# Taking GpSimd out of the last stores of an attention + MLP kernel

## The chip, the core and the metric

The kernel runs on one core of one Trainium2 chip. The metric is device time in microseconds (us) of that core, as the median of several executions. One further execution was recorded by the profiler. The engines are TensorE (PE, with its weight loads shown as PEld), VectorE (DVE), ScalarE (ACT), GpSimd (POOL) and SyncE (SP). SP, ACT and POOL can each issue DMA transfers.

## The reference

For 8 batches of 8 heads, 576 rows and head size 64, a Nystrom form of attention is computed. Its result, 4608 rows of 512, goes through a two-layer perceptron.

```python
q_lm = q.reshape(B, H, m, S // m, D).mean(axis=3)      # m = 32 landmarks
k_lm = k.reshape(B, H, m, S // m, D).mean(axis=3)
A = sm(q, k_lm); Bm = sm(q_lm, k_lm); C = sm(q_lm, k)  # scaled softmaxes
Z = Bm.transpose(0, 1, 3, 2) / (norm_1(Bm) * norm_inf(Bm) + 1e-06)
for _ in range(6):
    Z = 2 * Z - Z @ Bm @ Z
attn_out = A @ Z @ C @ v
x = attn_out.transpose(0, 2, 1, 3).reshape(B * S, H * D)
h = x @ w_in                                           # 4608 x 2048
out = (h * sigmoid(h)) @ w_out                         # 4608 x 512
```

## The kernel before

The kernel works batch by batch. For batch `b`, `attn(b)` builds the landmark softmaxes, the iteration for Z and a matrix `m` that already holds Z, C, v and `w_in`. `layer1(b)` multiplies `etn` (the normalised A) with `m`, 128 hidden columns at a time (`h0` to `h15`), and puts silu of the result into `gm` on ScalarE. Sixty-four of the 576 rows do not fit the 512-wide tile. They are gathered by two narrower groups per batch, `hx0` and `hx8`, each 16 matmuls of 64 columns, and their silu (`gx0`, `gx8`) goes to the tile `gx`. One `gx` holds four batches, so it is complete only when the two groups of the fourth batch are done.

`layer2_batch(b)` multiplies by `w_out`. Two blocks of 256 rows of `gm` are each done by `layer2_pair`, a seven-product scheme. The products are `p1` to `p7`, each 8 matmuls. DVE forms four sums of inputs beforehand (line 1028, tiles `ss` and the second half of the input). The results are collected in two output tiles `ost`, a low one and a high one, by copies and additions (`c1`, `c11`, `u2`, `c22`, `c12`, `c5`, `c21`). `p6`, `p7` and `p4` follow `p1` in its PSUM bank, each after the one before it has been read out (`c1`, `u2`, `c22`). The low tile needs `c11` (after `p2`) and `c12`; the high one `c21` (after `p4`) and `c22` (after `p7`). After batches 3 and 7 a third pair, the one on `gx`, follows. In batch 7 it is the end of the kernel.

Stores: each output tile holds four blocks of 32 rows, and each block goes out as one DMA of 64 KB (line 1005). Everywhere but in the last pair SP issues all of them. In the last pair (`spread`) they are single steps. The high tile goes in eight half stores of 32 KB that SP or ACT may issue, the low tile in four stores of 64 KB that SP, ACT or POOL may issue.

The order of everything is not written out. Each step is an `Op` with the engines that can do it, a planned duration, its dependencies and a rank `prio`, and `Plan.run` builds a list schedule when the kernel is built: at each event it gives an idle engine the ready step with the lowest rank that finds a PSUM bank. The engines then run these lists in order, synchronised by semaphores, so the plan fixes an order, not times. Ranks are 1000 + 100b + column for layer 1 (a half more for `hx`), and 5000 + 100b (+20, +40 for the second and third pair) for layer 2. The step name ends in that number, as in `p2@5740.0`. The dictionary `ORDER` at the top adds a shift to the rank of single steps; `hx0.6` is the group `hx0` of batch 6.

After the last step the Tile framework closes the program. SP waits for the semaphores of all transfers, every engine executes a DRAIN, and GpSimd collects the engines' signals, clears the semaphores and releases them. These instructions carry line 1185.

Of the kernel before, what the change touches and what calls it, by code (L numbers as in the profile page):

```python
# [29 lines left out]
    "m3.5": (1570.1, 0), "p2@5400.0": (14.101, 0), "p4@5400.0": (-0.02249, 0),  # L30
    "Ax11.6": (-36.172, 0), "Cx10.6": (565.87, 0), "p6@5500.0": (-0.10422, 0),
    "ltr1.7": (-211.67, 0), "pbs.7": (230.47, 0), "bbd.7": (541.69, 0), "Rs0.7": (163.07, 0),
    "etn1.7": (-1755.9, 0), "p2@5740.0": (89.123, 0),
}


# [277 lines left out]
def kernel(  # L314
# [9 lines left out]
    nc = tc.nc  # L324
# [84 lines left out]
    A = P.add  # L409
# [563 lines left out]
    ost_st = {}  # L973

    def layer2_plain(gm, c, deps, places, prio):

        pieces = []
        for h in range(2):
            cell = {}
            cols = slice(c + 128 * h, c + 128 * h + 128)  # L980
            for qt in range(4):
                def f(e, qt=qt, cell=cell, cols=cols):
                    for dc in range(4 * qt, 4 * qt + 4):
                        mm(bank(cell["o"]), gm[:, dc, cols], w_out_sb[:, dc, :], start=(dc == 0),
                           stop=(dc == NDC - 1))
                d = deps(4 * qt, 4 * qt + 4) + [wo_ops[qt]]
                o = A(f"o{qt}@{prio + h}", [("PE", mm_us(512, 4))], f,
                      d + ([(pieces[-1], 0.0)] if qt else []), prio + h + 0.01 * qt,
                      psum=0 if qt else 1, cls="L2")
                cell.setdefault("o", o)  # L990
                pieces.append(o)
            i = nost[0] % 6
            nost[0] += 1
            t = ost_r[i]
            a = A(f"oc@{prio + h}", either(512), lambda e, t=t, cell=cell: copy(
                e, t, bank(cell["o"])), [pieces[-1]] + ost_st.get(i, []),
                500.0 + prio / 100).reads(cell["o"])
            ost_st[i] = [A(f"os@{prio + h}", [("SP", 2.2)],
                           lambda e, t=t, h=h: [store(e, t, places[h], m) for m in range(4)],
                           [a], prio, dma=0.65, lag=3.5)]  # L1000
        return pieces

    def store(e, t, place, m, cols=slice(0, DMODEL)):
        b, j = place[m]
        {"SP": nc.sync, "ACT": nc.scalar, "POOL": nc.gpsimd}[e].dma_start(  # L1005
            out=out[b * S:(b + 1) * S, cols].rearrange("(l j) n -> j l n", j=J)[j],
            in_=t[L * m:L * m + L, cols])

    def layer2_pair(gm, c, deps, places, prio, parts=1, spread=False):
# [29 lines left out]
        def prod(nm, i, lhs, rhs, deps, own=None):  # L1039
            cell = {"o": own}  # L1040

            def f(e):
                ps = bank(cell["o"])[:, 0:HM]
                for dc in range(HC):
                    mm(ps, lhs[:, dc], rhs[:, dc], start=(own is None and dc == 0),
                       stop=(dc == HC - 1))
            o = A(f"{nm}@{prio}", [("PE", mm_us(HM, HC))], f, deps, prio + 0.01 * i,
                  psum=1 if own is None else 0, cls="L2")
            o.margin = 0.1
            o.pair = n  # L1050
            if own is None:
                cell["o"] = o
            pieces.append(o)
            return o
# [17 lines left out]
        p2 = prod("p2", 1, a12, b21, [p1] + deps(HC, NDC) + w2)  # L1072
# [16 lines left out]
        for i, t, h, dep in ((lo_i, lo_t, 0, [c11, c12]), (hi_i, hi_t, 1, [c21, c22])):  # L1089
            if spread and h:  # L1090
                ost_st[i] = [A(f"os{u}{m}@{prio + h}", [("SP", 0.45), ("ACT", 0.45)],
                               lambda e, m=m, t=t, u=u: store(e, t, places[1], m, slice(
                                   HM * u, HM * u + HM)), [dep[u]], prio + 0.1 * u,
                               dma=0.1, lag=1.5) for u in range(2) for m in range(4)]
            elif spread:
                ost_st[i] = [A(f"os{m}@{prio}", [("SP", 0.45), ("ACT", 0.45), ("POOL", 0.7)],
                               lambda e, m=m, t=t: store(e, t, places[0], m), dep, prio,
                               dma=0.1, lag=1.5) for m in range(4)]
            else:
                ost_st[i] = [A(f"os@{prio + h}", [("SP", 2.2)],  # L1100
                               lambda e, t=t, h=h: [store(e, t, places[h], m) for m in range(4)],
                               dep, prio, dma=0.65, lag=3.5)]
        return pieces

    def layer2_batch(b):
        l2_last["m", b] = []
        for p in range(2):
            x = (gm_r[b % 2], 256 * p, lambda d0, d1: gm_ops[b][d0:d1],
                 [[(b, j) for j in range(8 * c + p, 8 * c + p + 7, 2)] for c in range(2)],
                 5000.0 + 100 * b + 20 * p)  # L1110
            if b or p:
                l2_last["m", b] += layer2_pair(*x)
            else:
                l2_last["m", b] += layer2_plain(*x)
                w_sums(l2_last["m", b][:])
        if b % 4 == 3:
            l2_last["x", b // 4] = layer2_pair(
                gx_t, 0, lambda d0, d1: [gx_ops[x][d // 8] for x in range(b - 3, b + 1)
                                         for d in range(d0 // 8 * 8, d1, 8)],
                [[(x, j) for x in (y, y + 1) for j in (J - 2, J - 1)] for y in (b - 3, b - 1)],  # L1120
                5000.0 + 100 * b + 40, 1, b == B - 1)
# [68 lines left out]
```

## Time and profile before

| | |
|---|---|
| median of 9 runs | 253.29 us (252.84 to 254.27) |
| profiled execution: its own time | 254.27 us |
| its span, first to last instruction of the program | 252.6 us (252.57) |
| PE / ACT / DVE / POOL busy | 96% / 72% / 68% / 15% |
| mean granted TensorE clock | 0.995 |

The profile is of one execution, which was the slowest of the nine. 1.70 us of its time lie outside its span. Busy shares are averages over the whole span. In groups of instructions, the numbers after the bar are total busy time in us, the mean duration in ns, and the idle time before with what ended it. In the view of one source line, a row gives the duration in ns as minimum, median and maximum, and the first and last start in us. A "q" after an engine's name marks its sequencer (issues of transfers, waits, drains), which is not counted as busy.

### The profile page before, as it was taken

To read this page: it belongs to the slowest core of one execution; us is meant where nothing else is said; L and a number is where in the kernel's file an instruction comes from. 1 tells how busy PE (TensorE), PEld (TensorE's weight loads), DVE (VectorE), ACT (ScalarE), POOL (GpSimd) and SP (SyncE) were. 2 spreads that over 40 slices of the span, in tenths; PEclk is the share of its full clock that TensorE was granted. 3 is DMA by queue.
4 is the path that set the end of the run, shared out by engine and by line. 5 is a ranking of instruction groups with operands and counts; after the bars stand their busy time and mean duration, and the time that the engine had idled before them with its cause. 6 is when DMAs were issued, how large, how long until landed. Compare 5 with 4: busy or idle time off the path is not lost.

```text
span 252.6 us, 7198 instructions
## 1 busy us (share of the span) xinstructions
PE 241.4 (96%) x2846; PEld 173.4 (69%) x2846; DVE 170.9 (68%) x432; ACT 182.3 (72%) x429; POOL 37.8 (15%) x64
## 2 busy tenths in 40 slices
PE   7899999999989999999999999999999999999980
PEld 6777665556867754567886665788776685788870
DVE  2376766596879867949999674399996465257520
ACT  2598997499866999997768889678679977622210
POOL 8436724200040022001300130000000000000000
PEclk9999999999999999999999999999999999999997
DMA  6999999997989799994996999764340023033342
GB/s 104 205 193 199 204 207 208 206 239 124 163 164 214 123 187 193 162 166 93 171 239 136 207 167 215 133 136 114 84 110 0 22 67 83 0 86 84 86 108 58
DMA packets 52465, 35.73 MB, mean 141 GB/s; under 512 B 33376, under 2 KB 43872, under 8 KB 52432
## 3 DMA queue, kind: packets, MB, share of 16 engines
q0 software_dynamic: 15296, 18.42, 43.9%
q1 hardware_dynamic: 36800, 16.56, 30.4%
q8 instruction: 22, 0.36, 0.6%
q10 hardware_dynamic: 336, 0.30, 0.4%
q14 instruction: 11, 0.09, 0.1%
HBM read 36.70 MB, written 9.44 MB: 183 GB/s over the span
## 4 chain that ended last, share of the span: by engine, by line
issue 41%; PE 39%; DMA 9%; ACT 4%; DVE 2%; POOL 2%; SPq 1%; POOLq 0%; DVEq 0%; ACTq 0%
PE ps L392 37%; DMA qT<-qk 6%; DMA qk<-in_q_dram 3%; PE ps L566 2%; SPq L590 1%; DVE red L626 1%; ACT ln L778 1%; POOL v L458 1%; ACT ln L782 1%; PE ps L828 1%; ACT ct L402 1%; ACT et L768 1%; ACT L940 1%; POOL qk L451 0%; POOL qk L445 0%
## 5 line engine op out<-in xcount | busy, mean ns | idle before, releaser
L392 PE MATMUL ps<-etn,m 128*128 128x64 bf16 (+1 forms) x512 | 69.4, 286 | 0.1
L940 ACT ACTIVATE gm<-ps 128x512 f16<-128x512 f32 x128 | 66.1, 659 | 2.3 <-PE ps L392 2.1
L392 PEld LDWEIGHTS <-gm 128*128 128x128 f16 x512 | 48.2, 98 | 11.4 <-issue 2.6
L392 PE MATMUL ps<-w_out_sb,gm 128*128 128x256 f16 (+1 forms) x392 | 53.5, 281 | 0.0
L392 PEld LDWEIGHTS <-m 128*128 128x128 bf16 x512 | 32.5, 98 | 24.8 <-issue 2.6
L402 ACT COPY ost<-ps 128x256 f32<-128x256 f32 (+1 forms) x55 | 21.4, 389 | 32.1 <-PE ps L392 30.6
L392 PEld LDWEIGHTS <-ss 128*128 128x128 f16 x408 | 39.0, 98 | 7.2 <-issue 1.1
L1063 DVE TENSOR_TENSOR ost<-ost,ps 128x256 f32<-128x256 f32 x51 | 21.3, 418 | 23.3 <-PE ps L392 18.3
L392 PE MATMUL ps<-wt,ss 128*128 128x256 f16 x272 | 34.1, 273 | 0.0
L738 DVE SCALAR_TENSOR_TENSOR st<-st,ps 128x320 bf16<-128x320 bf16 (+3 forms) x54 | 21.6, 407 | 8.6 <-PE ps L392 8.3
L404 DVE CAST m<-ps 128x512 bf16<-128x512 f32 x31 | 20.0, 684 | 5.0 <-PE ps L392 4.5
L402 ACT CAST m<-ps 128x512 bf16<-128x512 f32 x33 | 17.8, 600 | 3.5 <-PE ps L392 3.5
L392 PE MATMUL ps<-w_out_sb,ss 128*128 128x256 f16 x136 | 17.6, 273 | 0.0
L451 POOL DMA_DIRECT2D qk<-in_k_dram x7 | 5.0, 717 | 82.2 <-DMA qT<-qk 37.9
L813 ACT ACTIVATE ce<-ps 128x288 bf16<-128x288 f32 x32 | 12.8, 412 | 5.2 <-PE ps L392 5.2
L392 PE MATMUL ps<-zer 128*128 128x256 bf16 x94 | 15.2, 296 | 1.1 <-DVE zer L485 1.1
L458 POOL DMA_DIRECT2D v<-in_v_dram x24 | 14.0, 592 | 14.9 <-PE ps L392 8.6
L392 PE MATMUL ps<-wt,gm 128*128 128x256 f16 x120 | 15.6, 273 | 0.0
L1005 POOL DMA_DIRECT2D out_dram<-ost x1 | 0.5, 528 | 98.8 <-DVE ost L1063 98.8
L392 PE MATMUL ps<-st 128*128 128x160 bf16 (+1 forms) x96 | 14.4, 225 | 0.4 <-DVE st L738 0.3
L1028 DVE TENSOR_TENSOR ss<-gm 128x1024 f16<-128x1024 f16 x15 | 10.2, 686 | 5.2 <-ACT gm L940 5.2
L626 DVE TENSOR_TENSOR red<-qT 128x1024 f16<-128x1024 bf16 x12 | 8.3, 689 | 7.9 <-DMA qT<-qk 7.4
(91 smaller groups left out, 339.7 us busy)
## 6 DMA issues: line engine op xcount, KB each, us to landing
out_dram<-ost SPq DMA_DIRECT2D x137, 64.0 KB, 1.8
v<-in_v_dram POOLq DMA_DIRECT2D x24, 192.0 KB, 12.2
qk<-in_k_dram POOLq DMA_DIRECT2D x7, 576.0 KB, 8.2
qk<-in_q_dram POOLq DMA_DIRECT2D x7, 576.0 KB, 11.6
w_out_sb<-in_moe_w_out_dram POOLq DMA_DIRECT2D x4, 512.0 KB, 10.5
w_in_sb<-in_moe_w_in_dram POOLq DMA_DIRECT2D x4, 256.0 KB, 9.1
w_in_sb<-in_moe_w_in_dram POOLq DMA_DIRECT2D x8, 128.0 KB, 7.3
qk<-in_k_dram POOLq DMA_DIRECT2D x2, 288.0 KB, 4.2
```

The costliest lines, as they stand in the source:

```text
L392: nc.tensor.matmul(out=out_ap, lhsT=lhsT, rhs=rhs, start=start, stop=stop, skip_group_check=True)
L402: nc.scalar.copy(out=out, in_=in_)
L404: nc.vector.tensor_copy(out=out, in_=in_)
L451: lambda e, t=t, src=src: nc.gpsimd.dma_start(out=qk_r[b % 2][:, t].rearrange("p g j d -> p g (j d)"), in_=src[b].rearrange("(g h) (l j) d ...
L458: lambda e, a=a: nc.gpsimd.dma_start(out=v_r[b % 2][a * L:(a + 1) * L, :, :], in_=v[b].rearrange("h (l a x) d -> a l h (x d)", l=L, a=VA)[ ...
L566: nc.tensor.transpose(out=ps[:, n * 128:(n + 1) * 128], in_=qk[:, t, g, 2 * jp:2 * jp + 2, :].rearrange("p j d -> p (j d)"), identity=idb)
L626: lambda e: nc.vector.tensor_tensor(out=o_, in0=a_, in1=b_, op=OP.add),
L738: nc.vector.scalar_tensor_tensor(out=s2[:, g0:g1, lo:SW], in0=s[:, g0:g1, lo:SW], scalar=2.0, in1=ps[:, 0:NG * SW].rearrange("p (g x) -> p ...
L813: nc.scalar.activation(out=ce[:, :, 0:VP].rearrange("p (i c) (a l) -> p c a i l", c=2, a=VA)[:, c], in_=bank(me["C"], 2 * g + c)[:, 0:HS]. ...
L940: lambda e, dc=dc, cell=cell: nc.scalar.activation(out=gm[:, dc, :], in_=bank(cell["o"]), func=AF.Silu),
L1028: lambda e, o_=o_[:, k], x=x[:, k], y=y[:, k], op=op: nc.vector.tensor_tensor(out=o_, in0=x, in1=y, op=op), dep, 850.0 + prio / 100)
L1063: nc.vector.tensor_tensor(out=out_, in0=x, in1=y, op=OP.add)
```

## The change

Two things are done in the diff. The low tile's four stores of the last pair may be issued by SP or ACT only; GpSimd is struck from the list of choices and from `store`. In `ORDER`, the step `hx0.6` gets a shift of 4199.5, so its rank goes from 1607.5 to 5807.0.

```diff
@@ ORDER
     "ltr1.7": (-211.67, 0), "pbs.7": (230.47, 0), "bbd.7": (541.69, 0), "Rs0.7": (163.07, 0),
-    "etn1.7": (-1755.9, 0), "p2@5740.0": (89.123, 0),
+    "etn1.7": (-1755.9, 0), "hx0.6": (4199.5, 0), "p2@5740.0": (89.123, 0),
 }
@@ store
         b, j = place[m]
-        {"SP": nc.sync, "ACT": nc.scalar, "POOL": nc.gpsimd}[e].dma_start(
+        {"SP": nc.sync, "ACT": nc.scalar}[e].dma_start(
             out=out[b * S:(b + 1) * S, cols].rearrange("(l j) n -> j l n", j=J)[j],
             in_=t[L * m:L * m + L, cols])
@@ layer2_pair
             elif spread:
-                ost_st[i] = [A(f"os{m}@{prio}", [("SP", 0.45), ("ACT", 0.45), ("POOL", 0.7)],
+                ost_st[i] = [A(f"os{m}@{prio}", [("SP", 0.45), ("ACT", 0.45)],
                                lambda e, m=m, t=t: store(e, t, places[0], m), dep, prio,
                                dma=0.1, lag=1.5) for m in range(4)]
```

## The prediction

> **What bounds the kernel now.** I read the page first, for what bounds the body, and then only the end, where the change lies: the timeline of the last engines, the closing line 1185, and the busy time in the last microseconds.
>
> ```profile
> span 252.6 us, 7198 instructions
> ...
> PE   7899999999989999999999999999999999999980
> ...
> PEclk9999999999999999999999999999999999999997
> DMA  6999999997989799994996999764340023033342
> ...
> L1005 POOL DMA_DIRECT2D out_dram<-ost x1 | 0.5, 528 | 98.8 <-DVE ost L1063 98.8
> ```
>
> The PE row is at nine tenths or more up to the last slices: the body is bound by TensorE, at full clock. The last row says that GpSimd issues exactly one of the stores, after having had nothing to do for 98.8 us.
>
> ```profile
> 242.16 0.37 ACT L402 COPY ost<-ps 128x256 f32<-128x256 f32 x1 [0.50 <-PE ps L392]
> ...
> 244.58 1.04 PE L392 MATMUL ps<-w_out_sb,gx 128*128 128x256 f16 x8
> 244.78 0.42 DVE L404 COPY ost<-ps 128x256 f32<-128x256 f32 x1 [0.45 <-PE ps L392]
> 245.65 0.42 DVE L1063 TENSOR_TENSOR ost<-ost,ps 128x256 f32<-128x256 f32 x1 [0.45 <-PE ps L392]
> 246.36 0.53 POOL L1005 DMA_DIRECT2D out_dram<-ost  x1 [98.80 <-DVE ost L1063]
> ```
>
> This is the timeline's end (start, length, engine). TensorE's last product ends at 245.6, the last addition (c11, on DVE) at 246.07, and then the low tile's four stores go out: ACT at 246.1, POOL at 246.36, SP at 246.5, ACT at 246.6. All arithmetic is over 6.5 us before the span is. What fills these 6.5 us is in the view of line 1185:
>
> ```profile
> L1185 SPq EVENT_SEMAPHORE  x11: 17/28/683, 246.9 to 252.5; - x11
> L1185 POOLq EVENT_SEMAPHORE  x4: 17/17/17, 251.8 to 252.5; - x4
> L1185 POOLq DRAIN  x3: 46/102/5445, 246.3 to 252.3; - x3
> L1185 SPq DRAIN  x3: 7/7/7, 249.1 to 252.0; - x3
> ```
>
> and in the busy time of the last stretches (PE, PEld, DVE, ACT, POOL, clock, DMA share, GB/s):
>
> ```profile
> 246.00:248.00 2.00, 0.00 (x0) 0.00 (x0) 0.07 (x1) 0.00 (x0) 0.53 (x1) 1.00 0.61 166
> 248.00:250.00 2.00, 0.00 (x0) 0.00 (x0) 0.00 (x0) 0.00 (x0) 0.00 (x0) 1.00 0.14 45
> 250.00:252.60 2.60, 0.00 (x0) 0.00 (x0) 0.00 (x0) 0.00 (x0) 0.00 (x0) 0.50 0.00 0
> ```
>
> SP waits for all transfers and reaches its DRAINs at 249.1 and 249.2. GpSimd's first DRAIN starts at 246.3, with the issue of its store, and lasts 5.445 us, to 251.8; only then come its semaphore instructions (first start 251.8) that release everybody. From 250 on no engine and no DMA does anything. So SP is ready at 249.2 and the core waits 2.6 us more, for GpSimd alone. The chain of waits does not show this: it ends at GpSimd's issue at 246.34, since it follows program work. GpSimd's other two DRAINs in that row took 0.102 and 0.046 us, and one at the program's head, on line 1174, 0.184 us. None of these follows a store by GpSimd.
>
> **The change, part by part.**
>
> GpSimd's store is removed. With it goes the 2.6 us: GpSimd's instruction before it is then its last load, issued by 147.57, and the DRAIN follows that. Bounds on when it ends: with the same 5.4 us, at 153; if it has to outlast the landing of these loads (12.2 us in the page's list of issues) by as much as it outlasted the store's landing (issue 246.36 plus 2.2 is 248.6; 251.8 is 3.2 later), at 163. Both are over 80 us before it is needed. From then on SP's second DRAIN is the last to come. After it I put what followed GpSimd's DRAIN before: 251.8 to 252.57, 0.8 us.
>
> The store is added to SP or ACT. Four stores of 64 KB on two queues are two each, so the added one stands behind another: SP's started at 246.5 and the next can start at about 246.94, since such issues take 0.42 us (median of SP's rows at the end) with some 0.04 between. Nothing waits behind it: ACT's last copy ran at 242.16, SP has only the closing waits. The bytes are the same, and the DMA share of 0.61 and then 0.14 has room. From issue to landing 64 KB took 1.8 us in the page's median and 2.4 at the most in the last 10 us, so it lands between 248.7 and 249.3. Before, the last landing was 248.95 (246.55 + 2.4), and SP's DRAIN came 0.25 later. This way SP would be done at 249.0 to 249.6.
>
> A rule speaks against this part. The Trainium skill, Perfetto Trace Analysis, section DMA Optimizations, says that where descriptor generation is the bottleneck, spreading DMAs over SP, ACT and GpSimd may help; here the stores do stand in a row. By the rule alone the change costs one issue, +0.4 us. By the trace it saves 2.6 and costs that 0.4: GpSimd's issue ended at 246.9 (246.36 + 0.53), no earlier than the last of the others at 247.0. I go with the trace.
>
> hx0.6 is moved. Its 16 matmuls (slots of about 0.47 us, as seen at 200.00 to 200.47) and one silu of 0.6 us (line 963) are the same work elsewhere. Removed near 194.8, they let the rest come 0.47 earlier. By its rank of 5807 it loses to every product of layer 2 but p2@5740.0 (5740.01 + 89.12), so it fills the first moment at which nothing else is ready. That is, I read, behind p1 of the pair 5720: there the trace before has p1 of the last pair at 234.10 (`w_out_sb,gx`), pulled ahead between two products of the other pair because nothing else was ready. But that p1 reads gx, which now lacks gx0.6. So hx0.6 takes this place (233.63 to 234.10), p2 of pair 5720 follows at 234.10, and p1 of the last pair comes after p4 of 5720, at 239.34. The products are 0.87 us each throughout, so seven of them end at 245.45, within the overlap of the pipeline where they ended before: cost zero, if no gap opens.
>
> The cover for that zero: gx0.6 at 234.2 to 234.8 on ACT, then four sums on DVE of 0.69 each (line 1028), 2.8 us, between the additions of pair 5720, so until about 238.5; p5, the first that needs a sum, starts at 240.2. And the three hand-overs in p1's bank (PE to ACT or DVE to PE, 0.09 + 0.42 + some 0.1, so 0.6) need a product of 0.87 between them: p1, p5, p6, p3, p7, p2, p4 is such an order, and the ranks give it. Without cover, each costs up to 0.6.
>
> With that order p4 comes last, not p2, since p2 fills the hand-over before p4. Then the low tile's 64 KB stores start already at 245.25, and the last four are halves of 32 KB, started from 246.1 in two rows of two, the last at 246.57. These land 1.6 us later in the trace, and up to 2.2 if they meet the big ones: 248.2 to 248.8, SP done at 248.4 to 249.05.
>
> The sum: SP done at 248.4 to 249.6 over both orders; I take 249.0, where they meet. Plus 0.8 gives a span of 249.8, against 252.57: 2.8 less. The profiled execution would take 254.27 - 2.8 = 251.5, but it was 0.98 above the median of the runs shown, so I set the gain against the median: 253.29 - 2.8 = 250.5.
>
> **The rivals.**
>
> The DRAIN is not the store's (slower). GpSimd pays 5.4 us of closing that can only begin once the last store of any engine is issued. Then it moves from 246.34 to the end of the added issue, 247.36 (246.94 + 0.42), ends at 252.8, 1.0 later than now: 254.3. It decides as soon as the DRAIN starts later than 246.34; it costs the gain in part as soon as it ends after 249.2. For it: the trace has only one long DRAIN, and it does coincide with the end. Against: it began before the stores of SP at 246.5 and ACT at 246.6 were issued, and the short ones. Chance 0.07.
>
> TensorE waits for the late gx. If hx0.6 falls behind the products of pair 5720, p1 stands until gx0.6 is there: 0.09 + 0.6 + 0.1, 0.8 us, and the sums may add a hand-over of 0.6 or so. Gain 2.8 - 1.4: 251.9 (251.3 with the 0.8 alone). For it: the rank is nearly the lowest of all. Against: the gap at 234.10. Chance 0.12.
>
> The semaphore of the added store is not free. Stores share a few semaphores, and before, SP stood 1.5 us in one such wait (`DMA out_dram<-ost: 1.5`, in SP's list of waits near the end). In the last row that puts the landing off by up to 1.2 us: 251.7. Chance 0.08.
>
> The change does not do what it says: the planner might hand the steps to queues otherwise, but no store can go to GpSimd any more; I give that no share.
>
> **How the numbers follow.** The likeliest case, the DRAIN out of the way and TensorE's end unmoved, has 0.71; its own range is 249.9 to 251.1 (SP done from 248.4 to 249.6). The two cases that eat part of the gain reach to 251.9 with 0.20; 0.07 lies at 254.3, and 0.02 at no change (a disorder that eats it all). For 8 in 10, with 0.2 added to both sides for the spread of medians, the range is 249.8 to 251.9. A measurement of this kernel can tell 0.2%, 0.5 us, from no change. Faster by more than that 0.91, within 0.02, slower 0.07.
>
> **What would show it.** Right: no GpSimd row on line 1005; a long or short GpSimd DRAIN that starts near 147, and its semaphore instruction within 0.1 us of SP's second DRAIN, near 249; the span's last stretch without work shrunk from 3.4 us to 0.8; 20 stores by SP and ACT from 239.9 on, where there were 19 and one by GpSimd; hx0.6 between p1 and p2 of pair 5720 near 233.6; PE's last product ending at 245.6 within 0.2. Wrong: a GpSimd DRAIN of some 5 us still at the end; an idle stretch before a PE product after 234 with `ACT gx` or `DVE ss` as the releaser; an SP semaphore wait of over 0.5 us before the last store.

## The result, and the profile after

| | before | after |
|---|---|---|
| median | 253.14 us (54 runs) | 250.96 us (17 runs) |
| ratio, with its 95% interval | | 0.9903 (0.9887 to 0.9919) |
| profiled execution: its time | 254.27 us | 251.53 us |
| its span | 252.57 us | 249.42 us |
| TensorE's last product ends | 245.61 us | 245.44 us |
| from there to the end of the span | 6.96 us | 3.98 us |
| its time outside the span | 1.70 us | 2.11 us |

The median is 0.46 us above the forecast of 250.5 and inside its range. The ratio is that of the means, 253.22 us before and 250.77 after: a gain of 2.46 us. The medians lie 2.18 apart.

Two rows of the changed kernel's page first, then its timeline of TensorE at the end (start, length, engine):

```profile
span 249.4 us, 7196 instructions
...
PE   8899999999989999998999999999999999999993
...
PEclk9999999999999999999999999999999999999998
```

```profile
233.46 0.63 PE L392 MATMUL ps<-etn,m 128*128 128x64 bf16 x16
...
238.30 1.04 PE L392 MATMUL ps<-w_out_sb,gx 128*128 128x256 f16 x8
239.17 1.04 PE L392 MATMUL ps<-wt,gm 128*128 128x256 f16 x8
...
244.41 1.04 PE L392 MATMUL ps<-w_out_sb,gx 128*128 128x256 f16 x8
```

TensorE is as full as before. hx0.6 (the 16 matmuls of 64 columns) runs at 233.46. p1 of the last pair follows at 238.30, one place ahead of p4 of the pair before it (239.17), and p2 is still the last product (244.41). Now the closing line 1185:

```profile
L1185 SPq EVENT_SEMAPHORE  x11: 17/28/28, 247.1 to 249.4; - x11
L1185 POOLq EVENT_SEMAPHORE  x4: 17/17/17, 248.7 to 249.3; - x4
L1185 POOLq DRAIN  x3: 51/102/16132, 146.1 to 249.1; - x3
L1185 SPq DRAIN  x3: 7/7/13, 248.6 to 248.9; - x3
```

GpSimd's long DRAIN starts at 146.1, with the issue of its last loads, and lasts 16.132 us, to 162.2, when nobody waits for it. SP's second DRAIN comes at 248.6, and GpSimd's semaphore instruction right after it, at 248.7. Before, 2.6 us lay between the two. SP's second DRAIN is now 0.77 us from the end of the span (248.65 to 249.42), where it was 3.36 (249.21 to 252.57). The busy time of the last stretches (columns as before: length, PE, PEld, DVE, ACT, POOL, clock, DMA share, GB/s) has no stretch of 2.6 us without any transfer any more; the last store lands at 248.50:

```profile
246.00:248.00 2.00, 0.00 (x0) 0.00 (x0) 0.00 (x0) 0.00 (x0) 0.00 (x0) 1.00 0.70 186
248.00:249.40 1.40, 0.00 (x0) 0.00 (x0) 0.00 (x0) 0.00 (x0) 0.00 (x0) 0.50 0.01 1
```

SP itself is also earlier: 3.21 us after TensorE's end (248.65 - 245.44) where it was 3.60 (249.21 - 245.61). The list of stores from 240 on says why:

```profile
L1005 SPq DMA_DIRECT2D out_dram<-ost x12: 314/401/435, 239.8 to 246.8; - x12
L1005 ACTq DMA_DIRECT2D out_dram<-ost x6: 374/410/435, 243.4 to 246.4; - x6
...
DMA to landing us min/median/max: 1.5/1.7/1.9
```

The last store is issued later (246.8, before 246.6), but no store takes more than 1.9 us to land; before it was up to 2.4.

### The profile page after: what moved, and what is told of

Read it like the earlier page. It is cut to its first block, busy times and chain, and to the rows that moved or that the text cites. A ratio compares the mean times of both kernels' runs of the same rounds, so it can differ in the third digit from the quotient of the medians.

```text
span 249.4 us, 7196 instructions
## 1 busy us (share of the span) xinstructions
PE 241.7 (97%) x2846; PEld 173.8 (70%) x2846; DVE 169.6 (68%) x430; ACT 182.8 (73%) x431; POOL 37.2 (15%) x63
## 3 DMA queue, kind: packets, MB, share of 16 engines
q0 software_dynamic: 15264, 18.35, 44.5%
## 4 chain that ended last, share of the span: by engine, by line
PE 86%; DMA 6%; ACT 3%; DVE 2%; issue 1%; POOL 0%; DVEq 0%; POOLq 0%; ACTq 0%
PE ps L392 83%; DMA qT<-qk 4%; DMA qk<-in_q_dram 3%; PE ps L566 2%; ACT ln L778 1%; DVE red L626 1%; ACT ln L782 1%; PE ps L828 1%; ACT ct L402 1%; ACT et L768 1%; ACT L940 1%; POOL qk L445 0%; DVE ost L1063 0%; ACT gm L940 0%; DVE ost L404 0%
## 5 line engine op out<-in xcount | busy, mean ns | idle before, releaser
L392 PE MATMUL ps<-etn,m 128*128 128x512 bf16 (+1 forms) x512 | 69.3, 286 | 0.1
L402 ACT COPY ost<-ps 128x256 f32<-128x256 f32 (+1 forms) x57 | 22.1, 388 | 33.8 <-PE ps L392 32.2
L392 PE MATMUL ps<-zer 128*128 128x256 bf16 x94 | 15.8, 304 | 1.1 <-DVE zer L485 1.1
L778 ACT ACTIVATE ln<-ps 128x288 f32<-128x288 f32 x32 | 12.0, 435 | 1.9 <-PE ps L392 1.7
```

What stands on the lines that cost most here:

```text
L392: nc.tensor.matmul(out=out_ap, lhsT=lhsT, rhs=rhs, start=start, stop=stop, skip_group_check=True)
L402: nc.scalar.copy(out=out, in_=in_)
L778: lambda e, g=g, c=c, ln=ln: nc.scalar.activation(out=ln[:, c], in_=bank(me["S", g, c])[:, 0:HS], func=AF.Ln),
```

## Which part of the change earns it

The end of TensorE differs by up to 2.3 us between profiles (243.7 to 246.0). The cause lies in the body, the part up to TensorE's last product, and was not looked for. So the variants are read by two lengths that hardly vary in kernels that share their end: the tail, from TensorE's last product to the end of the span, in the profile; and the time outside the span, device time less span, of every execution. Spans are recorded to 0.1 us, so a single time outside is good to 0.05. Each ratio is to executions of the kernel before that were made beside the variant. GpSimd kept awake has three executions, and the two with the late copy behind an added DRAIN and the kernel before with an early DRAIN have two each; the others have 4 to 17.

| kernel | tail, us | outside the span, us | ratio to before (95%) |
|---|---|---|---|
| before | 6.96 | 1.65 to 1.78 | |
| after | 3.98 | 2.06 to 2.16 | 0.9903 (0.9887 to 0.9919) |
| only hx0.6 moved | 6.95 | 2.08 to 2.16 | 1.0019 (0.9994 to 1.0045) |
| only GpSimd struck | 4.14 | 1.70 to 1.73 | 0.9893 (0.9846 to 0.9940) |
| GpSimd's store one pair earlier | 3.97 | 2.09 to 2.13 | 0.9903 (0.9869 to 0.9936) |
| late GpSimd copy | 6.36 | 2.06 to 2.15 | 0.9993 (0.9966 to 1.0020) |
| late copy, GpSimd kept awake | 6.49 | 2.04 to 2.07 | 0.9955 (0.9923 to 0.9987) |
| early DRAIN, late copy | 3.97 | 2.11 to 2.12 | 0.9894 (0.9866 to 0.9923) |
| DRAIN before the last 10 loads, late copy | 3.97 | 2.08 to 2.11 | 0.9889 (0.9798 to 0.9980) |
| before, with an early DRAIN | 4.36 | 1.68 to 1.74 | 0.9857 (0.9827 to 0.9886) |
| low tile in two stores | 10.68 | 2.00 to 2.03 | 1.0130 (1.0091 to 1.0169) |
| low tile in halves | 5.01 | 2.21 to 2.29 | 0.9937 (0.9912 to 0.9962) |
| halves, third queue, early DRAIN | 4.75 | 2.36 to 2.48 | 0.9949 (0.9920 to 0.9979) |
| after, again | 3.96 | 2.08 to 2.17 | 0.9914 (0.9882 to 0.9947) |

**Only hx0.6 moved.**

```diff
# against the kernel before
-    "etn1.7": (-1755.9, 0), "p2@5740.0": (89.123, 0),
+    "etn1.7": (-1755.9, 0), "hx0.6": (4199.5, 0), "p2@5740.0": (89.123, 0),
```

> Only hx0.6 is moved, GpSimd keeps its store. Theory D (the time is GpSimd's DRAIN after its own late store): no gain, ratio to before 0.998 to 1.002, a GpSimd DRAIN of 5.4 us from about 246.2 to 251.6 in the profile, span 252.4 (0.2 less by the slightly earlier end of TensorE). Rival H (the moved matmul group earns it, through TensorE's order): ratio 0.990.

Its GpSimd rows in line 1185:

```profile
L1185 POOLq EVENT_SEMAPHORE  x4: 17/17/17, 251.2 to 251.8; - x4
L1185 POOLq DRAIN  x3: 46/102/5443, 245.7 to 251.6; - x3
```

The tail is unchanged and so is the DRAIN: rival H is out. The spans agree too: their mean is 251.48 us over ten executions, and 251.50 over the 22 of the kernel before beside them. But the ratio leans to slower, without leaving 1 out of its interval, and the table shows where 0.4 us come from: outside the span, where the ten executions of this kernel lie at 2.08 to 2.16 and the 22 of before at 1.65 to 1.78.

**Only GpSimd struck from the stores** (the changed kernel without the entry for hx0.6).

> Only GpSimd is struck from the stores, hx0.6 stays. Theory D: nearly the whole gain, ratio 0.990 to 0.992, no late GpSimd DRAIN, SP's second DRAIN at 248.6 to 249.3, span 249.4 to 250.1. Rival H: ratio 1.000.

The tail is 4.14, the time outside that of before. This half alone brings the gain.

## What the DRAIN pays for

The prediction put the long DRAIN down to GpSimd's late store. Four theories were set against each other: D, it is a transfer of GpSimd that makes the DRAIN long; C, any late use of GpSimd's queue; W and S, GpSimd's late waking after 100 us of sleep; B, the first DRAIN pays for what all transfers since the last DRAIN left behind.

**GpSimd's store one pair earlier.** Three stores of the low tile of pair 5720 stay with SP, and GpSimd issues the fourth.

```diff
# against the changed kernel, in layer2_pair (store has GpSimd again)
+            elif prio == 5720.0 and not h:
+                ost_st[i] = [A(f"os@{prio}", [("SP", 1.65)],
+                               lambda e, t=t: [store(e, t, places[0], m) for m in range(3)],
...
+                             A(f"osp@{prio}", [("POOL", 0.7)],
+                               lambda e, t=t: store(e, t, places[0], 3), dep, prio,
```

> The changed kernel, but GpSimd issues one 64 KB store of the pair before the last one (at about 239), and none of the last pair. Theory D: the DRAIN starts at about 239, lasts about 5.4 us and is over near 245, before SP is done at 248.6: ratio 0.990, as the changed kernel. Rival C (a closing cost that any late use of GpSimd's queue brings at the end of the program): the DRAIN ends after SP's and the ratio goes back towards 1.000.

GpSimd's DRAINs in the closing line (1192 in this kernel):

```profile
L1192 POOLq DRAIN  x3: 46/102/5442, 238.6 to 248.5; - x3
```

The same 5.44 us, but begun at 238.6 and over at 244.0: the whole gain is kept. What counts is when the DRAIN begins, and it isn't a cost of the program's end: theory C falls.

**A late copy, no transfer.**

```diff
# against the changed kernel
+                A("late", [("POOL", 0.3)], lambda e: nc.gpsimd.tensor_copy(
+                    out=late, in_=lo_t[:, 0:32]), [c11], prio)
```

> The changed kernel with one small GpSimd copy (128 x 32 elements, SBUF to SBUF, no DMA, its result unused) after the last addition. Theory D (the DRAIN is long because of a transfer of GpSimd): the copy runs at about 246.2 and the DRAIN behind it lasts under 0.5 us: ratio 0.990. Rival W (it is long because GpSimd worked at all so late, or had slept 100 us): a DRAIN of some 5 us, ratio 1.000.

The copy in GpSimd's timeline, and the DRAIN in the view of the closing line, which is 1189 here:

```profile
246.53 0.21 POOL L1101 COPY late<-ost 128x32 f32<-128x32 f32 x1 [99.30 <-DVE ost L1065]
```

```profile
L1189 POOLq DRAIN  x3: 51/102/5056, 246.5 to 252.1; - x3
```

A copy of 0.21 us brings the long DRAIN back and takes nearly all of the tail's gain. Theory D falls: no late transfer is needed. W and B were left.

**GpSimd kept awake.** One such copy after c11 in each of the pairs of batches 6 and 7, and the late one.

> The late GpSimd copy of the run before, and four more such copies ahead of it, one per pair from about 218 on, so that GpSimd is never idle for 100 us before the last one. Theory S (the DRAIN is long because GpSimd had slept): a short last DRAIN, under 1 us, ratio 0.990. Theory B (the first DRAIN after GpSimd's transfers pays for something these left behind, whenever they were): still 4.8 us after the last copy, ratio 1.000.

The last two copies in GpSimd's timeline, and the DRAIN in its closing line:

```profile
234.16 0.54 POOL L1079 COPY late<-ost 128x32 f32<-128x32 f32 x1 [6.40 <-DVE ost L1065]
244.36 0.21 POOL L1104 COPY late<-ost 128x32 f32<-128x32 f32 x1 [9.65 <-DVE ost L1065]
```

```profile
L1192 POOLq DRAIN  x3: 51/102/5047, 244.3 to 249.9; - x3
```

GpSimd had slept 9.65 us, not 99, and the DRAIN is as long: sleep is not it. (The ratio of 0.9955 is better than the tail explains; TensorE ended at 243.7 in this profile. That lies in the body, and three executions don't settle whether it is chance.)

**An early DRAIN, then the late copy.**

```diff
# in attn, after the loads of the next batch are queued
+        if b == B - 1:
+            A("pdrain", [("POOL", 0.3)], lambda e: nc.gpsimd.drain(), v_ops[b], 0.0)
```

> A DRAIN of GpSimd right after its last load (about 147), then the same single late copy as before. Theory B: the early DRAIN pays, to about 162, and the last one, behind the copy, is under 0.5 us: ratio 0.990. Theory S or a fixed price of the closing DRAIN behind late work: 4.8 us again, ratio 1.000.

The copy ran at 245.66 for 0.209 us. The closing line:

```profile
L1191 POOLq DRAIN  x3: 39/102/303, 245.6 to 248.8; - x3
```

With one DRAIN at 145, the closing one is 0.303 us and the tail 3.97. Theory B holds: the price is that of the first DRAIN after GpSimd's transfers, whatever runs in between.

**The DRAIN before the last 10 loads** asks how the price grows: the same with `b == 5`, so that 48 of the 58 loads come before the added DRAIN and 10 after it.

> The late GpSimd copy, with an added DRAIN of GpSimd after 48 of its 58 loads, so that 10 loads lie between it and the closing DRAIN. If the price goes with the number of transfers since the last DRAIN (4.8 us for 58, 0.08 each): 0.8 us, over by 247, ratio 0.990. If any undrained transfer brings the whole price: 4.8 us again, ratio 1.000.

The closing line, with the copy of 0.209 us at 246.45 again:

```profile
L1191 POOLq DRAIN  x3: 51/102/1127, 246.4 to 249.6; - x3
```

The DRAIN's record starts with the instruction before it, so that one's length comes off. No transfer left: 303 - 209 = 94 ns. Ten: 1127 - 209 = 918. All 58: 5056 - 209 = 4847. With the store as the 59th, in the kernel before: 5445 - 528 = 4917. So 10 transfers cost 824 ns and 58 cost 4753: 82 ns for each since the last DRAIN, on top of 0.09 us. It goes by their number and not by their bytes: the one store of 64 KB added 70 ns, where its part of the price by bytes (the loads moved 18.35 MB) would be 17. GpSimd's own work adds nothing: with five copies the DRAIN took 5047 ns, with one 5056.

In these cases the loads had landed long before. A DRAIN that has to wait for a landing is left with half the price: in the changed kernel the last load lands at 159.82, and the DRAIN ends 2.42 us later, at 162.24. The seven other traces in which a DRAIN waits for the last of 58 loads have 2.42 too, and the added DRAIN of this run, behind 48 loads, has 2.01. That is 42 ns for each transfer. Why it is half, no run shows.

**The kernel before, with the early DRAIN.**

> The kernel before, with GpSimd's late store, and an added DRAIN of GpSimd right after its last load. Theory B, if one transfer leaves as much behind as all of them: 4.9 us after the store, ratio 1.000; if the price grows with the transfers since the last DRAIN: less, a DRAIN that ends with the store's landing at 248.6 or soon after, ratio 0.990 to 0.992. Theory S: 1.000.

The store was issued at 244.99, in 0.53 us. The closing line:

```profile
L1187 POOLq DRAIN  x3: 51/102/2280, 245.0 to 248.3; - x3
```

With only its own store to account for, the DRAIN lasts 2.28 us, to 247.25. That is 0.09 after this store's landing at 247.16 and before SP's 247.8. So GpSimd's store could have stayed: the tail falls to 4.36 with it. The ratio of 0.9857 is the best seen, but of two executions, and with a tail 0.4 longer than the changed kernel's the lead lies in the body (TensorE's end at 244.2), which varied as much between kernels that share it. Whether it is really faster stays open.

## Can the rest of the tail be shortened

**The low tile in two stores** of 128 KB, each two blocks of 32 rows.

```diff
# against the changed kernel: store2 is store with these lines, two neighbouring j at once
-            out=out[b * S:(b + 1) * S, cols].rearrange("(l j) n -> j l n", j=J)[j],
-            in_=t[L * m:L * m + L, cols])
+            out=out[b * S:(b + 1) * S, cols].rearrange("(l j) n -> j l n", j=J)[j:j + 2],
+            in_=t[L * m:L * m + 2 * L, cols])
```

> The changed kernel with the low tile of the last pair in two stores of 128 KB, one on SP and one on ACT, instead of four of 64 KB. If what is left of the end is the row of issues on SP and ACT and the last landing (248.5 in the changed kernel, its last store issued at 246.75 after a wait of 0.4 for a semaphore), both issues are at 246.0 and land near 248.0: 0.4 to 0.6 us off the end, ratio to before 0.988. If a bigger transfer takes longer to land by as much, the ratio stays at 0.990.

Busy time in stretches behind the last store (columns as above, DMA share and GB/s last):

```profile
248.00:250.00 2.00, 0.00 (x0) 0.00 (x0) 0.00 (x0) 0.00 (x0) 0.00 (x0) 0.96 0.12 28
250.00:252.00 2.00, 0.00 (x0) 0.00 (x0) 0.00 (x0) 0.00 (x0) 0.00 (x0) 0.50 0.14 36
252.00:254.00 2.00, 0.00 (x0) 0.00 (x0) 0.00 (x0) 0.00 (x0) 0.00 (x0) 0.50 0.12 45
```

A bad miss: the tail is 10.68 us. The DMA share is 0.12 to 0.14 of 16 engines, about 2 of them, at 28 to 45 GB/s, where the changed kernel had 0.70 and 186 GB/s between 246 and 248. The destination's access pattern now begins with a dimension of 2. The Trainium skill, DMA: Bandwidth & Descriptors, section "Why a DMA increments its semaphore by 16 and not by 1", says that a transfer is spread over the largest number of engines up to 16 that divides the first dimension over 1 of both its patterns. Here these are 64 rows in the tile and 2 in the destination, and the measured share of about 2 engines agrees. A store of 128 KB with another pattern was not run, so the size as a cause is set aside by this share alone.

**The low tile in halves**, the half after c12 sent ahead.

```diff
# against the changed kernel
-                ost_st[i] = [A(f"os{m}@{prio}", [("SP", 0.45), ("ACT", 0.45)],
-                               lambda e, m=m, t=t: store(e, t, places[0], m), dep, prio,
-                               dma=0.1, lag=1.5) for m in range(4)]
+                ost_st[i] = [A(f"os{u}{m}@{prio}", [("SP", 0.45), ("ACT", 0.45)],
+                               lambda e, m=m, t=t, u=u: store(e, t, places[0], m, slice(
+                                   HM * u, HM * u + HM)), [dep[u]], prio + 0.1 * (1 - u),
+                               dma=0.1, lag=1.5) for u in range(2) for m in range(4)]
```

> The changed kernel with the low tile of the last pair in eight stores of 32 KB, the four of the column half that is ready first (after c12) sent ahead. If the last 64 KB landings set the end, only halves are left after c11: about 0.25 us less from TensorE's last product to the end of the span (3.7 instead of 4.0). If the row of issues on SP and ACT sets it (16 instead of 12), 0 to 0.4 us more. The ratio to before, 0.988 to 0.992, can hardly tell; the profile can.

From SP's list of waits near the end (total, times, longest):

```profile
SPq L1005 <- DMA out_dram<-ost: 1.3, 1, 1.3
```

One microsecond more of tail, beyond either expectation. Four more issues of some 0.4 us and this wait for a store's semaphore put the last issue at 247.60, against 246.75 in the changed kernel.

**Halves with GpSimd as third queue, and the early DRAIN.**

> The stores in halves, with GpSimd again allowed to issue of the low tile's, and the early DRAIN after GpSimd's last load. Two of the eight go to GpSimd. If the early DRAIN takes the whole price, the closing one ends with the landing of GpSimd's own last store, near 247.5, and the third queue shortens the row of issues by up to 0.4 us: 3.6 us from TensorE's end to the end of the span, ratio 0.988. If GpSimd's stores land later than the others, no gain over two queues: 4.0 us, ratio 0.990.

The tail is 4.75: 0.26 less than two queues for the same 16 stores, and 0.8 more than 12 stores on two queues. GpSimd's closing DRAIN ended at 247.39 and was not in the way. Here fewer issues are worth more than a third issuer.

**The changed kernel again**, beside them:

> The changed kernel, unaltered, on the chip of the two variants of its stores, to compare them with: ratio 0.990, 4.0 us from TensorE's end to the end of the span.

Tail 3.96, ratio 0.9914, as expected. No variant tried has a tail shorter by more than 0.02.

## Why the prediction was right, step by step

- **GpSimd's DRAIN out of the way: right.** It begins at 146.1 and ends at 162.2; the bounds given were 153 and 163. GpSimd's signal follows SP's within 0.1 us, as foretold, and the 20 stores by SP and ACT are there, though from 238.9 on.
- **What makes the DRAIN long: wrong.** "None of these follows a store by GpSimd" took the nearest event for the cause. The late copy and the early DRAIN show that the 58 loads before make it long; the late store only fixed when it began. The sum stood by luck: by either reading, taking the store away moves the beginning to about 147.
- **The added store: the size was off.** SP was put at 249.0 to 249.6 for the order that in fact came; it was 248.65. The wait for a semaphore happened (0.4 us on SP, of the rival's 1.2), and the last issue was at 246.75, not 246.94, as TensorE ended 0.17 earlier. What was over-estimated is the landing, 1.75 us after issue and not 1.8 to 2.4, and the 0.25 from there to SP's DRAIN, which was 0.15. All three profiles with GpSimd among the last four stores have 2.2 to 2.4 for the last one (before, hx0.6 alone, the early DRAIN), the eight with four 64 KB stores on two queues 1.74 to 1.94. That the third queue does it was not tried apart. The rule of spreading the issues, which the prediction set aside, earned nothing for these 12 stores: with hx0.6 in its old place and no long DRAIN at the end, SP reached its second DRAIN 3.6 us after TensorE's end with GpSimd's store (early DRAIN) and 3.4 without (GpSimd struck). GpSimd's issue had ended at 246.89, the last of the others at 246.99: it was 0.1 earlier, where the prediction reads "no earlier".
- **hx0.6 fills the gap at 233.6 and costs no TensorE time: right.** It ran at 233.46, and the rows on line 1028 end at 237.7, against the 238.5 allowed. TensorE's end moved by 0.17, which says little where profiles differ by 2.3; the stronger evidence is hx0.6 alone, with a mean span of 251.48 against 251.50 (standard error of the difference about 0.3) and a tail of 6.95 against 6.96.
- **The order of the last pair: wrong.** p1 went ahead of p4 of pair 5720, so no hand-over was left for p2 to fill, and p2 stayed last. The halves did not end the kernel. It cost nothing, since the landings were quicker than assumed.
- **The time around the span, taken as 1.70: wrong by 0.4.** This is the term that nearly cancels the other misses, and that it does is luck. The tail gave 2.98, the time outside took 0.41 back: 2.57, measured 2.46. All kernels with the moved hx0.6 have about 2.0 or more outside; the three without (before, GpSimd struck, before with the early DRAIN) have 1.65 to 1.78.
- **The range: not the sum that is given for it.** The cases named for it reach from 249.9 to 251.9; with 0.2 on both sides that is 249.7 to 252.1, not 249.8 to 251.9. The result lies inside either.

By these terms, striking GpSimd without moving hx0.6 is worth 2.82 (6.96 - 4.14) with nothing given back, 0.25 more than the whole change. The measured ratios, 0.9893 and 0.9903, lean that way and don't separate the two.

## What to carry to other kernels

When a span ends in microseconds without work, look at the closing instructions of each engine and ask what each of them waited for and when it could have begun; the chain of program work doesn't show it. Where GpSimd has issued many transfers, its last instruction, of any kind, should come well before the end, or a DRAIN should stand where it hurts nobody. This is GpSimd's alone in these traces: SP issued over 140 stores, and its closing DRAINs took 7 to 13 ns. Before blaming the nearest event, change its kind and not only its place: moving the store earlier fitted the wrong theory as well as the right one, and the copy alone told them apart.

## What the runs showed that was not expected

- GpSimd's DRAIN costs 0.09 us plus 0.082 us for each of its transfers since its last DRAIN, though they had all landed over 80 us before. Where it had to wait for their landing, it ended 0.042 us for each transfer after the last one.
- Moving one group of matmuls in the program, with the tail as before, goes with 0.4 us more outside the span, in every execution (2.08 to 2.16 against 1.65 to 1.78). The variants of the stores went up to 2.48. What happens there no profile row shows, and it was not taken apart.
- Two stores whose destination pattern begins with a dimension of 2 moved at 28 to 45 GB/s together, and cost 6.7 us of tail.
